# Who scales the probabilities and takes the sign bits: VectorE's work handed to GpSimd in an attention and two-layer feed-forward kernel

## The chip, the core and the metric

The kernel runs on one core of one Trainium2 chip. Every time below is device microseconds (us) of one execution; the figure of merit is the median of several executions. Engines are called as the profile calls them: PE is TensorE (PEld its weight loads), DVE is VectorE, ACT is ScalarE, POOL is GpSimd, SP is SyncE, which here only issues DMAs.

## What is computed

Two batches of 768 positions, 8 heads of 64: attention inside a band (the 96 last positions and 8 global ones) with a linear bias, then two feed-forward layers on the 1536 tokens, 512 wide, with 2048 hidden units. In the reference, cut to what matters:

```python
scores = scale * np.matmul(q, k.transpose(0, 1, 3, 2)) + bias      # kept where keep, else -1e9
scores = scores - np.max(scores, axis=-1, keepdims=True)
a = np.exp(scores)
a = a / (np.sum(a, axis=-1, keepdims=True) + 1e-09)
x = np.matmul(a, v)
h = np.maximum(x @ w_in, 0.0);  x = h * h @ w_out                  # layer 0
h = x @ w_in2;  g = np.where(h >= 1, h, np.where(h <= -1, 0.0, (h + 1) ** 2 / 4))
out = g @ w_out2                                                   # layer 1
```

The weights arrive as 64-bit floats. [...]

## The kernel before

**The order is planned.** The program records every operation with the engines that may do it, an estimated duration and a due time, and `Plan.emit` (L184) then simulates the engines by those estimates and writes the instructions out in the order in which the simulation started them. Nothing is decided when the program runs: each engine takes its list in order and waits on semaphores. Three rules of `emit` matter here. An operation that several engines can do goes to the one that the plan thinks done first. VectorE and GpSimd share one path to SBUF in the plan: an operation flagged `port` may not start before `port`, the end of the last flagged one, so that no two of them ever overlap. And where the plan sees TensorE idle for longer than FGAP = 300 ns in the early part, it puts in **fillers**, matmuls on a tile of zeros (`warm`, recorded at L1342 until the first feed-forward product, at L1344 after it) whose result nobody reads.

**Attention.** The 12 blocks of 128 queries are done in halves of four heads (`BandAttention.half`). A half is: products of q and k (L868), four times "add the mask, keep the minimum" on VectorE (L890) and the exponential with its sum on ScalarE (L895), the addition of 1e-9 to the four sums (L900) and their reciprocal (L902) on VectorE, four multiplications of the probabilities by it (`Plan.scale`: L153 on ScalarE, L155 on VectorE, L157 on GpSimd), transposes on TensorE (L918), their copies out of PSUM (L129, L130), and the products with v (L954). Probabilities and sums have three buffers (`pr`, `mn`), so that consecutive halves overlap.

**Weights.** A chunk is 128 hidden units of both matrices, loaded as two DMAs into one of two `raw` buffers (L462). Each half of it becomes 32-bit floats in `whole` by four operations (`Ffn.float32`): ScalarE multiplies the high words, read as floats, by 2^-112 (L153); VectorE shifts the result left by 3 (L470), puts in the top three bits of the low words (L473) and then the sign bits of the high words (L477). A copy to the reduced format of the matmuls (ScalarE, L129) and a subtraction for the rest (VectorE, L140) give the two parts of a slot. A `raw` buffer is free for its next DMA when L477 has read it. All 16 chunks of layer 0 are made while attention runs, those of layer 1 later (`prepare`, L492), for storage in HBM.

**Order of the large loops.** The first 8 halves of attention come alone; from about the ninth on, the feed-forward of finished tokens (L535, L733; at first in pieces of 256 tokens) runs in between; then layer 0 for the rest, then layer 1 (L652, with its own products).

```python
            if ways[engine][2]:
                t = max(t, port)
                port = t + ns
```

## Time and profile before

| | us |
|---|---|
| median of 3 runs (lowest to highest) | 614.76 (613.58 to 614.92) |
| the profiled execution | 613.96 |
| its span, first to last instruction | 612.2 |

| engine | busy us of the span | share |
|---|---|---|
| PE | 599.7 | 98% |
| DVE | 481.0 | 79% |
| ACT | 351.5 | 57% |
| POOL | 58.1 | 9% |

The profiled execution lies 1.8 us above its span and 0.8 us below the median. A busy share is an average over stages that have different limits, so it has to be read together with a table by stage. A busy TensorE is also not yet a useful one: the fillers count as busy.

### The profile page before, as it was taken

The page shows a single profiled execution, that of the slowest core. Times are in us where ns is not written, and L with a number is a line of the kernel's source. Part 1 is how long each engine was busy: PE and PEld are TensorE (multiplying, and loading weights), DVE is VectorE, ACT ScalarE, POOL GpSimd, SP SyncE. Part 2 cuts the span into 40 slices and gives each one's busy share as a digit, 9 for nine tenths or more (in the row PEclk, how much of TensorE's full clock was granted, in tenths as well). Part 3 has the DMA queues.
Part 4 walks back from the last instruction along what each step waited for, and adds up shares of the span by engine and source line. Part 5 has one row for each costly group of instructions (what it writes and reads, how often), then busy time and mean ns, then how long its engine had stood idle before and what let it go on. Part 6 is the DMA issues. An engine that isn't in the chain of part 4 may idle for free. (4 is left out here: it accounts for less than half of the span.)

```text
span 612.2 us, 9673 instructions
## 1 busy us (share of the span) xinstructions
PE 599.7 (98%) x3438; PEld 514.0 (84%) x3438; DVE 481.0 (79%) x1031; ACT 351.5 (57%) x731; POOL 58.1 (9%) x88
## 2 busy tenths in 40 slices
PE   8999999999999999999999999999999999999995
PEld 5778987878888888888888898888899999888884
DVE  7999999965638988898566389999897788887862
ACT  7898877765547766674447464545553444444331
POOL 4120111010001104233200000000000000000000
PEclk9999999999999999999999999999999999999999
DMA  8553544430114879988512202323220022223002
GB/s 303 166 185 118 186 147 154 150 121 22 38 36 124 272 235 304 359 321 283 193 68 70 94 27 69 118 73 107 82 96 1 35 104 96 96 94 96 26 2 108
DMA packets 25790, 79.24 MB, mean 129 GB/s; under 512 B 2948, under 2 KB 2948, under 8 KB 25732
## 3 DMA queue, kind: packets, MB, share of 16 engines
q1 hardware_dynamic: 25730, 78.52, 38.0%
q8 instruction: 29, 0.48, 0.3%
q14 instruction: 29, 0.24, 0.1%
q10 hardware_dynamic: 2, 0.00, 0.0%
HBM read 62.78 MB, written 15.73 MB: 128 GB/s over the span
## 5 line engine op out<-in xcount | busy, mean ns | idle before, releaser
L658 DVE TENSOR_TENSOR pr<-bank,pr 128x384 f32<-128x384 f32 x112 | 60.2, 554 | 23.4 <-PE bank L652 22.5
L140 DVE TENSOR_TENSOR g<-r,g 128x512 fp32r<-128x512 f32 (+2 forms) x74 | 48.9, 660 | 34.7 <-ACT g L129 33.8
L550 ACT ACTIVATE r<-bank 128x512 f32<-128x512 f32 (+1 forms) x52 | 29.2, 562 | 59.7 <-PE bank L535 58.9
L129 ACT ACTIVATE g<-r 128x512 fp32r<-128x512 f32 (+2 forms) x74 | 42.7, 577 | 24.9 <-DVE r L567 14.2
L895 ACT ACTIVATE pr<-pr,mn 128x256 f32<-128x256 f32 (+1 forms) x96 | 45.9, 480 | 4.6 <-DVE mn L890 4.2
L563 ACT ACTIVATE r<-pr,small 128x384 f32<-128x384 f32 x43 | 26.2, 615 | 32.8 <-DVE pr L658 32.7
L153 ACT ACTIVATE whole<-raw 128x512 f32<-128x512 f32 x52 | 33.9, 668 | 9.1 <-DMA raw<-in_moe_w_out_dram 3.2
L477 DVE SCALAR_TENSOR_TENSOR whole<-raw,whole 128x512 uint32<-128x512 uint32 x52 | 36.7, 712 | 0.4
L890 DVE CUSTOM_DVE_ANT_0 pr<-bank,m 128x256 f32<-128x256 f32 (+1 forms) x96 | 33.4, 397 | 4.2 <-PE bank L954 4.1
L473 DVE SCALAR_TENSOR_TENSOR whole<-raw,whole 128x512 uint32<-128x512 uint32 x52 | 35.9, 702 | 0.3
L157 POOL TENSOR_SCALAR pr<-pr,mn 128x256 f32<-128x256 f32 (+1 forms) x38 | 21.4, 570 | 120.3 <-DVE mn L902 57.9
L868 PEld LDWEIGHTS bank<-nat,nat 64*128 64x128 f32 x352 | 22.7, 190 | 7.6 <-issue 2.7
L565 DVE SCALAR_TENSOR_TENSOR r<-r 128x384 f32<-128x384 f32 x43 | 23.8, 556 | 5.9 <-ACT r L563 5.1
L868 PE MATMUL bank<-nat,nat 64*128 64x128 f32 x352 | 27.0, 288 | 1.3 <-DVE mn L890 1.2
L563 ACT ACTIVATE nat<-pr,small 128x384 f32<-128x384 f32 x21 | 12.9, 617 | 24.5 <-DVE pr L658 24.5
L470 DVE TENSOR_SCALAR whole<-whole 128x512 uint32<-128x512 uint32 x52 | 22.9, 448 | 4.0 <-ACT whole L153 3.7
L129 ACT ACTIVATE pr<-bank 128x512 f32<-128x512 f32 (+2 forms) x46 | 23.5, 521 | 3.4 <-PE bank L652 2.1
L567 DVE TENSOR_TENSOR r<-pr,r 128x384 f32<-128x384 f32 x43 | 23.8, 557 | 1.2
L954 PE MATMUL bank<-pr,nat 128*64 128x128 f32 x352 | 24.0, 277 | 0.6 <-DVE mn L890 0.3
L918 PE MATMUL bank<-ident,pr 128*128 128x128 f32 x176 | 23.9, 275 | 0.0
L954 PEld LDWEIGHTS bank<-pr,nat 128*64 128x64 f32 x352 | 19.7, 136 | 4.8 <-issue 2.0
L918 PEld LDWEIGHTS bank<-ident,pr 128*128 128x128 f32 x176 | 20.0, 140 | 2.8 <-issue 0.5
(347 smaller groups left out, 1753.6 us busy)
## 6 DMA issues: line engine op xcount, KB each, us to landing
raw<-in_moe_w_in_dram SPq DMA_DIRECT2D x32, 512.0 KB, 4.4
raw<-in_moe_w_out_dram SPq DMA_DIRECT2D x32, 512.0 KB, 4.8
whole<-sums SPq DMA_DIRECT2D x14, 512.0 KB, 3.3
kept<-whole SPq DMA_DIRECT2D x12, 512.0 KB, 6.3
whole<-kept SPq DMA_DIRECT2D x12, 512.0 KB, 3.3
whole<-kept SPq DMA_DIRECT2D x13, 384.0 KB, 3.1
sums<-pr SPq DMA_DIRECT2D x8, 512.0 KB, 5.8
nat<-in_k_dram SPq DMA_DIRECT2D x12, 256.0 KB, 3.7
```

The source lines that it names most:

```text
L129: ("act", ns_act(n) - 30 * psum, lambda: nc.scalar.activation(out=at(out), in_=in_, func=ACTF.Copy), False),
L140: ways = [("dve", ns_dve(n), lambda: nc.vector.tensor_tensor(out=at(out), in0=in_, in1=at(hi).bitcast(F32), op=ALU.subtract), not psum)]
L153: ("act", ns_act(n) + (0 if isinstance(by, float) else 107), lambda: nc.scalar.activation(out=out, in_=in_, func=ACTF.Copy, scale=by), False),
L473: op("dve", ns_dve(512), d + 0.2, lambda h=h: nc.vector.scalar_tensor_tensor(out=word[:, h], in0=low[:, h], scalar=29, in1=word[:, h], op0 ...
L477: op("dve", ns_dve(512), d + 0.3, lambda h=h: nc.vector.scalar_tensor_tensor(out=word[:, h], in0=high[:, h], scalar=0x80000000, in1=word[: ...
L563: op("act", ns_act(N) + 64, due, lambda: nc.scalar.activation(out=r, in_=h, func=ACTF.Relu, bias=self.half, scale=0.5), keys, [kr])
L658: op("dve", ns_dve(W), start + step[name] + 0.2 - G_LEAD, lambda: nc.vector.tensor_tensor(out=to, in0=area[kb], in1=in1, op=ALU.add), [("b ...
L868: nc.tensor.matmul(**c)
L890: op("dve", ns_dve(w), due, lambda e=e: nc.vector.tensor_tensor_reduce(out=pr[:, e, :w], in0=self.banks[kbs[e % 2]][:, e // 2 * 256:e // 2 ...
L895: op("act", ns_act(w) + 200, due, lambda e=e: nc.scalar.activation(out=pr[:, e, :w], in_=pr[:, e, :w], func=ACTF.Exp, bias=mn[:, e:e + 1], ...
L918: self.nc.tensor.transpose(self.banks[kbs[m]][:, o:o + P], pr[:, 2 * m + e, c * P:(c + 1) * P], self.ident)
L954: nc.tensor.matmul(**c)
```

## The change

The plan no longer keeps VectorE and GpSimd apart. A flagged operation of GpSimd is planned 1.3 times as long (SHARE) and marks its end in `port`; a flagged operation of VectorE that starts before that end is planned longer by what is left of it, at most 90 ns (GIVE). The rule by which VectorE passed over a flagged operation (PASS) is gone. Three pieces of work move: from block 2 on (half 4 on) all four multiplications of a half are GpSimd's, where ScalarE, VectorE and GpSimd shared them; the 1e-9 is added by GpSimd; and the sign bits are taken by GpSimd. For the last one the four operations on a half chunk become: ScalarE's as before; GpSimd multiplies the high words by 0.0, which leaves a zero with the sign, in place in `raw`; VectorE combines that with the top bits of the low words, in place in `raw`; VectorE shifts ScalarE's result by 3 and combines it with that. VectorE has two operations per half chunk where it had three.

```diff
-SCALE, SCALE0 = ("act", "dve", "pool"), ("dve", "pool")
-CONV = ("act",)
+SCALE, SCALE0 = ("pool",), ("dve", "pool")
+CONV, SIGN = ("act",), ("pool",)
...
-                    others = max(free[e], t, port if ways[e][2] else 0)
-                    own = max(t, port if ways[engine][2] else 0)
+                    others, own = max(free[e], t), t
...
             if ways[engine][2]:
-                t = max(t, port)
-                port = t + ns
+                if engine == "pool":
+                    ns *= SHARE
+                    port = t + ns
+                elif engine == "dve" and port > t:
+                    ns += min(GIVE, port - t)
...
-            op("dve", ns_dve(256), d + 0.1, lambda h=h: nc.vector.tensor_scalar(
-                out=word[:, h], in0=word[:, h], scalar1=3, scalar2=None, op0=ALU.logical_shift_left,
-            ), (), [(*kc, n)], port=True)
+            self.plan.scale(512, d, high[:, h].bitcast(F32), high[:, h].bitcast(F32), 0.0, [(*kc, n)], [(*kr, n)], engines=SIGN)
             op("dve", ns_dve(512), d + 0.2, lambda h=h: nc.vector.scalar_tensor_tensor(
-                out=word[:, h], in0=low[:, h], scalar=29, in1=word[:, h],
+                out=low[:, h], in0=low[:, h], scalar=29, in1=high[:, h],
                 op0=ALU.logical_shift_right, op1=ALU.bitwise_or,
-            ), [(*kr, n)], [(*kc, n)], port=True)
+            ), (), [(*kr, n)], port=True)
             op("dve", ns_dve(512), d + 0.3, lambda h=h: nc.vector.scalar_tensor_tensor(
-                out=word[:, h], in0=high[:, h], scalar=0x80000000, in1=word[:, h],
-                op0=ALU.bitwise_and, op1=ALU.bitwise_or,
+                out=word[:, h], in0=word[:, h], scalar=3, in1=low[:, h],
+                op0=ALU.logical_shift_left, op1=ALU.bitwise_or,
             ), [(*kr, n)], [(*kc, n)], port=True)
...
-        op("dve", 70, due + 0.1, lambda: nc.vector.tensor_scalar(
-            out=mn[:, 4:8], in0=mn[:, 4:8], scalar1=1e-9, scalar2=None, op0=ALU.add), (), sums, port=True)
+        op("pool", 150, due + 0.1, lambda: nc.gpsimd.tensor_scalar(
+            out=mn[:, 4:8], in0=mn[:, 4:8], scalar1=1e-9, scalar2=1.0, op0=ALU.add, op1=ALU.mult), (), sums)
```

Since the plan simulates with new costs, all engines get a new order. Three places of it follow. Line numbers of the changed kernel are 6 to 8 lower than those of before (L527 for L535, L725 for L733, L860 for L868, L892 and L894 for L900 and L902).

GpSimd, from the second half of block 1 on. `pr<-pr,mn` is a multiplication of probabilities (mn_77, 78 and 79 are the three buffers of the sums), `nat` a small copy of keys. Before:

```order
L157 TENSOR_SCALAR pr<-pr,mn_77 128x256 x3
L133 TENSOR_SCALAR nat_125<-nat_125 128x4x32
L157 TENSOR_SCALAR pr<-pr,mn_78 128x256 x3
L157 TENSOR_SCALAR pr<-pr,mn_79 128x256
L157 TENSOR_SCALAR pr<-pr,mn_77 128x256
```

Now, with the sign operations (`raw<-raw`) and the additions (`mn<-mn`) in the same queue:

```order
L157 TENSOR_SCALAR pr<-pr,mn_77 128x256 x2
L157 TENSOR_SCALAR raw_116<-raw_116 128x512
L157 TENSOR_SCALAR raw_117<-raw_117 128x512 x2
L157 TENSOR_SCALAR raw_116<-raw_116 128x512 x2
L157 TENSOR_SCALAR raw_117<-raw_117 128x512
L133 TENSOR_SCALAR nat_125<-nat_125 128x4x32
L892 TENSOR_SCALAR mn_78<-mn_78 128x4
L157 TENSOR_SCALAR pr<-pr,mn_78 128x256 x3
L892 TENSOR_SCALAR mn_79<-mn_79 128x4
```

One to three multiplications of a half have become four, and six sign operations stand before the first addition of block 2.

TensorE, after the first feed-forward product of chunk 1 (`slot1`), on 256 tokens. Before:

```order
L535 MATMUL bank_63<-x,slot1l 128x256
L535 MATMUL bank_63<-x,slot1h 128x256 x2
L535 MATMUL bank_63<-x,slot1l 128x256
L535 MATMUL bank_63<-x,slot1h 128x256
L1344 LDWEIGHTS warm
L1344 MATMUL bank_63<-warm 128x256
```

Now:

```order
L527 MATMUL bank_63<-x,slot1l 128x256
L527 MATMUL bank_63<-x,slot1h 128x256
L725 MATMUL bank_65<-g_120,slot0h 128x256
L725 MATMUL bank_65<-g_120,slot0l 128x256
L725 MATMUL bank_65<-g_120,slot0h 128x256
L725 MATMUL bank_66<-g_120,slot0h 128x256
```

Nine fillers in a row stood there before, and 21 at L1344 in all; now the second product of chunk 0 (`slot0`) follows, and of the later fillers two are left. The earlier ones, at L1342, go from 31 to 35.

SP, the loads of block 5 (`in_q`, `in_k`, `in_v`) beside those of a weight chunk. Before:

```order
L841 DMA nat_125<-in_k_dram 128x512
L841 DMA nat_127<-in_v_dram 128x512
L841 DMA nat_126<-in_q_dram 128x512
L965 DMA nat_127<-in_v_dram 32x512
L462 DMA raw_117<-in_moe_w_in_dram 128x1024
L462 DMA raw_117<-in_moe_w_out_dram 128x1024
```

Now:

```order
L456 DMA raw_117<-in_moe_w_in_dram 128x1024
L456 DMA raw_117<-in_moe_w_out_dram 128x1024
L833 DMA nat_126<-in_q_dram 128x512
L833 DMA nat_125<-in_k_dram 128x512
L833 DMA nat_127<-in_v_dram 128x512
```

The two weight DMAs, which wait until VectorE has done with `raw`, have moved ahead of the loads of block 5.

## Rows read from the trace of the kernel before

**Rows 1.** Busy time by stage (windows; columns in the second line).

```profile
core 0: us, PE busy (x) PEld busy (x) DVE busy (x) ACT busy (x) POOL busy (x), PEclk, DMA share, GB/s
0.00:21.60 21.60, 18.69 (x161) 13.38 (x161) 16.61 (x74) 16.63 (x55) 8.40 (x25) 1.00 0.67 239
21.60:55.00 33.40, 30.96 (x305) 26.57 (x304) 30.88 (x101) 28.37 (x81) 6.13 (x10) 1.00 0.56 188
55.00:75.00 20.00, 20.00 (x196) 18.93 (x195) 19.48 (x63) 17.17 (x51) 2.11 (x4) 1.00 0.46 154
75.00:125.00 50.00, 50.00 (x371) 40.28 (x369) 48.21 (x133) 37.61 (x99) 5.93 (x10) 1.00 0.47 150
125.00:605.00 480.00, 480.00 (x2414) 414.80 (x2412) 365.43 (x663) 251.35 (x446) 35.56 (x39) 1.00 0.35 118
605.00:612.20 7.20, 0.02 (x1) 0.00 (x0) 0.42 (x1) 0.38 (x1) 0.00 (x0) 0.86 0.27 97
```

**Rows 2.** The same windows for the tile `warm` alone: the fillers.

```profile
21.60:55.00 33.40, 3.40 (x23) 1.87 (x21) 0.00 (x0) 1.00 0.56 188
```

**Rows 3.** TensorE in order of time: start, length, operation, count, the wait before it.

```profile
31.02 0.60 PE L1344 MATMUL bank<-warm 128*128 128x256 bf16 x4 [0.47 <-ACT r L550]
32.20 0.38 PE L1344 MATMUL bank<-warm 128*128 128x256 bf16 x2 [0.59 <-DVE r L552]
33.77 0.83 PE L1344 MATMUL bank<-warm 128*128 128x256 bf16 x6
36.76 1.25 PE L918 MATMUL bank<-ident,pr 128*128 128x128 f32 x8
56.78 1.42 PE L868 MATMUL bank<-nat,nat 64*128 64x128 f32 x16
```

**Rows 4.** Groups of DVE, 21.6 to 55 us (count | busy us, mean ns | idle before).

```profile
L473 DVE SCALAR_TENSOR_TENSOR whole<-raw,whole 128x512 uint32<-128x512 uint32 x7 | 4.8, 686 | 0.0
L477 DVE SCALAR_TENSOR_TENSOR whole<-raw,whole 128x512 uint32<-128x512 uint32 x6 | 4.1, 677 | 0.0
L470 DVE TENSOR_SCALAR whole<-whole 128x512 uint32<-128x512 uint32 x6 | 2.5, 419 | 0.0
L155 DVE TENSOR_SCALAR pr<-pr,mn 128x256 f32<-128x256 f32 x4 | 1.6, 404 | 0.0
L140 DVE TENSOR_TENSOR slot3l<-whole,slot3h 128x512 fp32r<-128x512 f32 x2 | 1.4, 690 | 0.0
L900 DVE TENSOR_SCALAR mn<-mn 128x4 f32<-128x4 f32 x5 | 0.8, 166 | 0.1
```

**Rows 5.** Groups of POOL and ACT in the same stretch.

```profile
L157 POOL TENSOR_SCALAR pr<-pr,mn 128x256 f32<-128x256 f32 x8 | 5.3, 666 | 16.8 <-DVE mn L902 16.8
...
L153 ACT ACTIVATE pr<-pr,mn 128x256 f32<-128x256 f32 x8 | 3.6, 498 | 0.9 <-DVE mn L902 0.9
```

**Rows 6.** POOL in order of time: multiplications and a small copy, at three places.

```profile
9.43 0.74 POOL L157 TENSOR_SCALAR pr<-pr,mn 128x128 f32<-128x128 f32 x2 [0.61 <-DVE mn L902]
10.29 0.30 POOL L133 TENSOR_SCALAR nat<-nat 128x128 f32<-128x128 f32 x1
34.37 0.94 POOL L157 TENSOR_SCALAR pr<-pr,mn 128x256 f32<-128x256 f32 x1 [2.80 <-DVE mn L902]
57.12 0.54 POOL L157 TENSOR_SCALAR pr<-pr,mn 128x256 f32<-128x256 f32 x1 [5.48 <-ACT pr L129]
```

**Rows 7.** DVE in order of time, around the third row of group 6.

```profile
34.03 0.17 DVE L902 RECIPROCAL mn<-mn 128x4 f32<-128x4 f32 x1
34.12 0.66 DVE L477 SCALAR_TENSOR_TENSOR whole<-raw,whole 128x512 uint32<-128x512 uint32 x1
34.70 0.35 DVE L155 TENSOR_SCALAR pr<-pr,mn 128x256 f32<-128x256 f32 x1
34.96 0.88 DVE L140 TENSOR_TENSOR slot1l<-whole,slot1h 128x512 fp32r<-128x512 f32 x1
```

**Rows 8.** POOL and DVE in order of time, near 241 us.

```profile
240.56 1.12 POOL L503 TENSOR_TENSOR pr<-whole,whole 128x256 f32<-128x256 f32 x1 [8.32 <-DVE whole L477]
...
241.11 1.11 DVE L477 SCALAR_TENSOR_TENSOR whole<-raw,whole 128x512 uint32<-128x512 uint32 x1
```

**Rows 9.** SP's queue in order of time: the load of q of block 5.

```profile
41.84 0.43 SPq L841 DMA_DIRECT2D nat<-in_q_dram  x1
```

More of the change, by code (lines that the diff above doesn't have):

```diff
@@ L44 @@
 FROM = 25
-PASS = 1.0
+SHARE, GIVE = 1.3, 90
 HOLD, NEAR = 0.5, 1
@@ L219, in emit @@
             i = heapq.heappop(a)[1]
-            if port > t and engine == "dve" and ops[i][0]["dve"][2]:
-                other = min(((d, j) for d, j in a if not by[j] and not ops[j][0]["dve"][2]), default=None)
-                if other and other[0] < ops[i][1] + PASS:
-                    heapq.heappush(a, (ops[i][1], i))
-                    a.remove(other)
-                    heapq.heapify(a)
-                    i = other[1]
             if engine in ("act", "dve", "pool") and HOLD:
```

## The prediction

> **What bounds the kernel now.** I read the table by stage first. From 55 to 605 us TensorE is busy in every microsecond, at a granted clock of 1.00 [rows 1]: 550 of the 612.2 us are a solid block of matmuls which the change neither adds to nor takes from, so whatever VectorE, ScalarE or GpSimd gain there buys nothing as long as TensorE stays fed. From 605 us the last tiles leave; nothing of the change is there. What is left is the first 55 us. From 0 to 21.6 us TensorE is busy for 18.69, in good part with fillers, and from 21.6 to 55 us for 30.96 of 33.40 [rows 1], of which 3.40 are fillers again [rows 2]. So in that second stretch 33.40 - 30.96 + 3.40 = 5.8 us do no work. That is the purse this change can draw on. The reader is to see in the same table what TensorE is short of there: VectorE is at 30.88 of 33.40 us, ScalarE at 28.37, GpSimd at 6.13 [rows 1]. The waits say the same: fillers stand behind a ScalarE operation (0.47 us) and a VectorE one (0.59 us) of the feed-forward [rows 3]; the attention and weight work queued on these two engines holds up the next products. From 75 to 125 us VectorE is as full, 48.21 of 50.00, but TensorE has longer pieces of work there and doesn't wait [rows 1].
>
> **The change, part by part, for 21.6 to 55 us.**
>
> Off VectorE: the shift, 2.5 us; the multiplications, 1.6 us; the addition of 1e-9, 0.8 us [rows 4]: 4.9 us of 30.88. The two operations that stay on a half chunk are of the kind and size of the two that cost 686 and 677 ns [rows 4], so I give them the same. Off ScalarE: eight multiplications, 3.6 us of 28.37 [rows 5].
>
> Onto GpSimd: 4 + 8 multiplications beside its own 8 [rows 4, 5], six sign operations and five additions. An undisturbed multiplication of 128x256 takes 0.54 us and one of 128x128 half of 0.74 = 0.37 us [rows 6]. Going on by that step, a sign operation of 128x512 is 0.54 + 2 x 0.17 = 0.88 us (an estimate; ends 0.54, if size cost nothing, and 1.08, if it cost all). An addition on 128x4 lies between nothing and the 0.30 us of the small copy [rows 6]; I take 0.25, by its nearness to that row. Sum: 20 x 0.54 + 6 x 0.88 + 5 x 0.25 = 17.3 us of 33.4, about 52% busy where it was 18%. GpSimd has room for it as a queue.
>
> What GpSimd's work costs VectorE is not idle time but collisions. In the trace a GpSimd multiplication that starts at 34.37 while VectorE is in L477 (until 34.78) takes 0.94 instead of 0.54 us [rows 6, 7]; the VectorE subtraction that meets its end (34.96) takes 0.88 [rows 7] where its like takes 0.69 [rows 4], so 0.19 more. A longer, two-input GpSimd operation at 240.56 makes L477 1.11 us [rows 8] instead of 0.68, so 0.43 more. I read that as one at a time for operations with two SBUF inputs: 240.56 + 1.12 = 241.68 is GpSimd's end, and L477, begun at 241.11, ends 0.54 later. The Trainium skill says the same (SBUF — State Buffer, section "SBUF: two separate sides"): the pair of ports that VectorE and GpSimd share is an exclusive lock, and the loser waits in full. By that rule the plan's 90 ns (GIVE) is too little, and the new order is packed too tightly.
>
> How often? VectorE keeps some 23 such operations in the stretch (7 + 6 at L473 and L477 [rows 4], by which there are about 7 slot subtractions at L140, and I add 3 for the hidden layer). With GpSimd busy for 52% of the time, about 12 meet it. Two thirds of GpSimd's busy time are multiplications, one third signs: 8 x 0.19 + 4 x 0.43 = 3.2 us. At 90 ns each it would be 1.1 us. So VectorE's net relief is 4.9 - 3.2 = 1.7 us by the collisions that the rows show, and 3.8 us by the plan's allowance. Its ends are 4.9 us (no collision) and 4.9 - 23 x 0.43 = -5.0 us (every one, at the dear price). ScalarE's 3.6 us come without collisions, and TensorE waits for it as often as for VectorE. **I take -2.0 us** for the stretch, a little over VectorE's own 1.7 for what ScalarE adds, out of the 5.8 us of purse. The order shows where it would be collected: 19 of the 21 late fillers are gone, and six of them took 0.83 us, 0.14 each [rows 3], so 2.6 us of them.
>
> **From 0 to 21.6 us.** Here the first eight halves run alone and TensorE follows the chain scores, exponential, reciprocal, multiplication, transposes. The multiplications there keep their two engines; the addition goes to GpSimd and adds a trip: at 34.03 + 0.17 = 34.20 the reciprocal ends and GpSimd starts at 34.37 [rows 6, 7], 0.17 us for a handover, so about +0.17 and +0.25 - 0.17 for the longer operation, 0.25 us per half. The first sign operations come late in this stretch, before the last multiplications, and are about 0.46 us longer than the shift they replace. Against that VectorE sheds a few shifts and additions. The order puts in 35 early fillers for 31: four of 0.14 us [rows 3]. **I take +0.5 us**, with ends -0.7 (four additions of 0.17 us saved on the chain) and +1.5 (0.25 us on each of four halves that nothing covers, and 0.46 for the first chunk).
>
> **From 55 us on: 0.** VectorE sheds the same three kinds of work there and meets GpSimd as often; TensorE is full, and the cover is that weights and hidden tiles are made ahead of it. If that cover went, each late half chunk would show as TensorE idle time, which no row of before has. SP: the two weight DMAs now stand ahead of block 5's loads, behind VectorE's release of `raw`. In the trace that q is issued at 41.84 [rows 9] and first used at 56.78 [rows 3], 15 us; VectorE would have to be late by most of that, so I cost it at nothing. The sign operations of layer 1's weights come while TensorE is in layer 0, which doesn't read them.
>
> Sum: -2.0 + 0.5 = **-1.5 us**. Against the profiled execution's 613.96 us (span 612.2) that is **612.5 us**; this execution lies 0.8 us under the median of 614.76, so on the median's scale the same sum is 613.3.
>
> A cost that no row of before shows is VectorE writing every second word (`raw`, in place). Reading every second word costs nothing: L473 reads `raw` so and takes 686 ns, the dense L140 690 [rows 4]. I take nothing for the write as well. The Trainium skill speaks against it (Vector Engine (DVE) Microarchitecture Reference, section "Measured stream behaviour on trn2"): full rate wants runs of two adjacent words, and single words cost about 0.65 cycle per element on reading and writing alike. By that rule the read in L473 should have been dearer too, which the row denies; a write at the page's price would be an estimated 0.35 us more per operation, 2.1 us for six, and would eat the gain.
>
> **Rivals.**
>
> *The plan is right and the purse is nearly emptied.* If collisions cost VectorE what the plan allows or less, the order holds, and the stretch gives up to VectorE's 4.9 us: -4.9 + 0.5, so 609.6 us. For it: the order, with two late fillers left. Against it: the 0.19 and 0.43 us of [rows 7, 8].
>
> *The relief is eaten.* Collisions, or the strided write, cost VectorE all that it sheds; fillers turn into plain waits of the same length: 0 + 0.5 in the first stage, at 614.0 to 614.5 us. For it: the exclusive use that the rows show. Against it: ScalarE's share.
>
> *Slower: GpSimd as the only scaler is late, and the transposes wait.* Four multiplications of a half now follow each other; the order was made with 1.3 x 457 = 594 ns for one (the plan's formula). Undisturbed they take 0.54, disturbed 0.94 us [rows 6]; at the middle, 0.75, a half is 4 x 0.15 = 0.6 us later than planned. In before, the shared multiplications ended at 34.37 + 0.94 = 35.31 [rows 6] and the transposes began at 36.76 [rows 3], a margin of 1.45 us, but the new order has no fillers left to take up lateness. Five halves of the stretch at 0.6 us are +3.1 us: -2.0 + 0.5 + 3.1 gives 615.6 us; at 0.94 throughout it would be 619. It decides from a mean multiplication of about 0.66 us on, where 5 x 4 x 0.07 = 1.4 us eat the gain. The mean in this stretch before, with few neighbours, is already 666 ns [rows 5].
>
> That the change doesn't do what it says can be left out: the order shows the moved operations.
>
> **How the numbers follow.** The forecast has 0.38, the emptied purse 0.22, the eaten relief 0.16, the slower case 0.24. A measurement of this kernel can tell about 0.2%, 1.2 us, from no change. The forecast's 1.5 us is just beyond that, so 0.29 of its 0.38 count as faster and 0.09 as the same; with the purse 0.51 faster, with the eaten relief 0.25 the same, 0.24 slower. The range: down to 609.5, the emptied purse; up to 616.0, which takes in the middle of the slower case and leaves out its dear end.
>
> **What would show it.** Right: from 21.6 to 55 us fewer fillers, TensorE's waits there no longer than before, VectorE near 29 us for the same work, L157 near 0.65 us, the block after 55 us still without a gap, and the end of the first stage up to half a us later. The first rival: VectorE's two-input operations at 0.69 on average despite GpSimd. The slower one: TensorE or its weight loads waiting at L910 for GpSimd's L157, and gaps after 55 us. A mean of the first VectorE operation on `raw` (L465) much above 0.69 us with no GpSimd beside it would show the strided write. The prediction is wrong if the time that moves lies after 55 us, or in the first stage by more than 1.5 us.

## The result and the profile after

The changed kernel takes **621.72 us** (median of 6 executions, 620.13 to 626.39), the kernel before 614.49 us on the same chip (6 executions, 613.58 to 614.92): a ratio of **1.0133, 95% interval 1.0106 to 1.0161**. It is slower, by about 7 us. The forecast was 612.5 us with a range of 609.5 to 616.0: wrong in sign, and outside its range. The profiled execution took 621.39 us with a span of 619.5, 7.3 us more than the 612.2 of before.

The table by stage answers to [rows 1]; its columns are the same (time and number of instructions per engine, then TensorE's granted clock, DMA share, GB/s).

```profile
0.00:21.60 21.60, 19.69 (x162) 14.08 (x163) 15.65 (x68) 16.30 (x53) 12.25 (x31) 1.00 0.71 253
21.60:55.00 33.40, 28.56 (x263) 24.52 (x261) 30.73 (x83) 25.60 (x71) 20.26 (x31) 0.95 0.54 169
55.00:75.00 20.00, 19.94 (x206) 18.51 (x205) 19.41 (x55) 16.57 (x47) 13.61 (x20) 1.00 0.66 215
75.00:125.00 50.00, 49.92 (x362) 40.06 (x362) 37.47 (x107) 33.55 (x94) 24.98 (x41) 1.00 0.42 143
125.00:605.00 480.00, 476.93 (x2404) 410.47 (x2403) 357.51 (x612) 247.10 (x436) 70.90 (x96) 1.00 0.35 115
```

Two things are new. The block after 55 us has gaps: 476.93 of 480.00 in its long row, where before it was 480.00. And from 21.6 to 55 us the granted clock is 0.95. The same view in steps of 25 us shows the place of the gaps:

```profile
200.00:225.00 25.00, 25.00 (x112) 20.68 (x111) 21.98 (x30) 17.70 (x31) 10.20 (x12) 1.00 0.70 232
225.00:250.00 25.00, 23.33 (x102) 18.67 (x100) 18.23 (x26) 14.44 (x24) 8.30 (x10) 1.00 0.79 255
250.00:275.00 25.00, 23.86 (x104) 19.41 (x105) 20.25 (x27) 13.77 (x22) 15.90 (x18) 1.00 0.97 331
275.00:300.00 25.00, 24.73 (x108) 19.86 (x107) 23.58 (x37) 14.86 (x27) 13.74 (x15) 1.00 0.93 319
```

A full window holds 112 matmuls, 25/112 = 0.223 us each. The three windows hold 10 + 8 + 4 = 22 too few: **4.9 us**. (Counted as idle time it is only 1.67 + 1.14 + 0.27 = 3.1 us, since the profile models where a matmul ends; the weight loads, which show the gaps too, waited for 5.2.) The other part of the loss lies ahead of it. The attention's products of probabilities with v are the last of the attention; the view of one line shows when the first and the last of them start, here in the kernel before and then in the changed one (operation, count, min/median/max ns, first and last start):

```profile
L954 PE MATMUL bank<-pr,nat x352: 272/273/323, 11.2 to 171.0; 128*64 128x128 f32 x176
```

```profile
L946 PE MATMUL bank<-pr,nat x352: 272/273/324, 12.2 to 173.6; 128*64 128x128 f32 x176
```

So **2.6 us** are lost by 173 us, 4.9 from 225 to 300, and 2.6 + 4.9 = 7.5 is within 0.2 us of the 7.3 of the span.

**What TensorE waits for from 225 to 300 us.** The waits of PE in 200 to 300 us of the changed kernel are a single row (total in us, times, longest), and its weight loads have the same one:

```profile
PE bank L725 <- DVE g L140: 3.1, 4, 1.2
```

```profile
PEld bank L725 <- DVE g L140: 5.2, 5, 1.6
```

`g` is the hidden tile that the second product of the feed-forward reads; VectorE's subtraction makes its low half. One such place in order of time (start, length, operation, count, idle before and what ended it):

```profile
225.03 1.84 POOL L157 TENSOR_SCALAR raw<-raw 128x512 f32<-128x512 f32 x2 [2.25 <-ACT whole L153]
225.23 1.13 DVE L469 SCALAR_TENSOR_TENSOR m<-m,raw 128x512 uint32<-128x512 uint32 x1
225.87 0.39 PE L725 MATMUL bank<-g,slot7l 128*128 128x512 f32 x1
226.28 1.12 DVE L140 TENSOR_TENSOR g<-r,g 128x512 fp32r<-128x512 f32 x1
227.46 0.72 PE L725 MATMUL bank<-g,slot7h 128*128 128x512 f32 x2 [1.20 <-DVE g L140]
```

GpSimd makes sign bits from 225.03 to 226.87. A weight step of VectorE (L469) meets them and takes 1.13 us in place of 0.68; behind it in VectorE's list stands `g`, which meets them too and takes 1.12; TensorE stands for 1.20 us. The weight step was in no hurry: TensorE first reads the slot that it is made for (slot6) at 264.75. The groups of VectorE over the whole span have the meetings in their means (count | busy, mean ns | idle before). L465 and L469 are VectorE's two steps on a half chunk, L140 is the subtraction. Operations of their kind and size took 677 to 690 ns from 21.6 to 55 us of before [rows 4], and over its whole span 702 (L473), 712 (L477) and, for `g`, 757.

```profile
L465 DVE SCALAR_TENSOR_TENSOR raw<-raw 128x512 uint32<-128x512 uint32 x64 | 52.0, 827 | 15.1 <-POOL raw L157 15.0
L469 DVE SCALAR_TENSOR_TENSOR whole<-whole,raw 128x512 uint32<-128x512 uint32 x52 | 37.5, 736 | 1.0
L140 DVE TENSOR_TENSOR g<-r,g 128x512 fp32r<-128x512 f32 x44 | 35.5, 808 | 21.8 <-ACT g L129 21.2
```

The first row also shows a wait that the kernel before doesn't have: 15.0 us in which VectorE, which takes its list in order, stands until a sign step is done.

That `g` is slow is not enough for a hole, though. The same group from 225 to 300 us alone, in the kernel before, in the changed one and in give_all, an experiment told below (the same kernel with another price in the plan, and no holes):

```profile
L140 DVE TENSOR_TENSOR g<-r,g 128x512 fp32r<-128x512 f32 x14 | 12.0, 857 | 8.1 <-ACT g L129 8.0
L140 DVE TENSOR_TENSOR g<-r,g 128x512 fp32r<-128x512 f32 x14 | 13.1, 938 | 0.0
L140 DVE TENSOR_TENSOR g<-r,g 128x512 fp32r<-128x512 f32 x14 | 11.5, 823 | 4.6 <-ACT g L129 4.6
```

The kernel before has slow ones too, at 857 ns on average, but there VectorE was early: it stood 8.0 us waiting for ScalarE's half of `g`. In the changed kernel it never waits for that half (0.0). It comes to each of the 14 only after that half is ready, since other work stands ahead of it in its list.

**What happens ahead of 55 us.** The first feed-forward product starts at 23.81 us, where it was 21.64 before. In order of time, in the changed kernel:

```profile
18.68 2.78 POOL L157 TENSOR_SCALAR raw<-raw 128x512 f32<-128x512 f32 x3
19.81 2.19 DVE L465 SCALAR_TENSOR_TENSOR raw<-raw 128x512 uint32<-128x512 uint32 x2 [0.56 <-POOL raw L157]
21.93 0.68 DVE L469 SCALAR_TENSOR_TENSOR whole<-whole,raw 128x512 uint32<-128x512 uint32 x1
22.64 0.63 ACT L129 ACTIVATE slot0h<-whole 128x512 fp32r<-128x512 f32 x1 [1.92 <-DVE whole L469]
23.18 0.58 ACT L129 ACTIVATE x<-bank 128x512 fp32r<-128x512 f32 x1
23.81 0.39 PE L527 MATMUL bank<-x,slot0h 128*128 128x256 f32 x1 [1.70 <-ACT x L129]
```

Three sign steps in a row on GpSimd, two VectorE steps that take 2.19 us beside them (at 686 ns each [rows 4] it would be 1.4), ScalarE standing 1.92 us for them with a tile of x queued behind, and TensorE 1.70 us for that. Then the clock (same columns as the table by stage):

```profile
21.60:24.00 2.40, 0.70 (x6) 0.39 (x5) 2.40 (x5) 1.27 (x3) 0.00 (x0) 1.00 0.30 72
24.20:27.60 3.40, 3.18 (x17) 2.85 (x18) 2.65 (x5) 1.37 (x4) 1.01 (x1) 0.53 0.93 296
27.60:55.00 27.40, 24.48 (x244) 21.18 (x242) 25.48 (x75) 22.76 (x66) 19.25 (x30) 1.00 0.51 163
```

After the gap (0.70 us busy of 2.40) the granted clock is 0.53 on average over 3.4 us, its lower level (1.2 GHz) for nearly all of them: by an estimate 0.47 x 3.4 = 1.6 us lost. The late fillers, on the other hand, nearly went: 0.90 us of them from 21.6 to 55 us against 3.40 [rows 2].

```profile
21.60:55.00 33.40, 0.90 (x7) 0.31 (x5) 0.00 (x0) 0.95 0.54 169
```

So the late start (2.2) and the clock (1.6) stand against 2.5 us of fillers saved: 1.3 us lost. The 1.3 us that are left to the 2.6 were not traced one by one. TensorE has further waits from 21 to 56 us: 1.0 us for GpSimd's multiplications (at L910), 0.9 for VectorE's mask step and 0.9 for the low half of a slot. The first of them, over the whole span (total, times, longest):

```profile
PE bank L910 <- POOL pr L157: 1.3, 3, 0.7
```

### The profile page after: what moved, and what is told of

It reads as the page before. It is cut to its first block, busy times and chain, and to the rows that moved or that the text cites. A ratio compares the mean times of both kernels' runs of the same rounds, so it can differ in the third digit from the quotient of the medians.

```text
span 619.5 us, 9731 instructions
## 1 busy us (share of the span) xinstructions
PE 602.5 (97%) x3423; PEld 513.5 (83%) x3423; DVE 463.9 (75%) x928; ACT 341.9 (55%) x704; POOL 142.0 (23%) x218
## 5 line engine op out<-in xcount | busy, mean ns | idle before, releaser
L140 DVE TENSOR_TENSOR g<-r,g 128x512 fp32r<-128x512 f32 (+2 forms) x74 | 51.6, 697 | 25.5 <-ACT g L129 24.8
L157 POOL TENSOR_SCALAR raw<-raw 128x512 f32<-128x512 f32 x64 | 50.0, 791 | 76.2 <-ACT whole L153 54.0
L465 DVE SCALAR_TENSOR_TENSOR raw<-raw 128x512 uint32<-128x512 uint32 x64 | 52.0, 827 | 15.1 <-POOL raw L157 15.0
L157 POOL TENSOR_SCALAR pr<-pr,mn 128x256 f32<-128x256 f32 (+1 forms) x88 | 56.5, 658 | 10.4 <-DVE mn L894 9.8
L469 DVE SCALAR_TENSOR_TENSOR whole<-whole,raw 128x512 uint32<-128x512 uint32 x52 | 37.5, 736 | 1.0
L860 PEld LDWEIGHTS bank<-nat,nat 64*128 64x128 f32 x352 | 23.3, 196 | 6.3 <-issue 3.9
L557 DVE SCALAR_TENSOR_TENSOR r<-r 128x384 f32<-128x384 f32 x43 | 23.8, 556 | 5.9 <-ACT r L555 5.1
L860 PE MATMUL bank<-nat,nat 64*128 64x128 f32 x352 | 27.9, 295 | 0.1
L910 PE MATMUL bank<-ident,pr 128*128 128x128 f32 x176 | 25.3, 277 | 1.5 <-POOL pr L157 1.3
L910 PEld LDWEIGHTS bank<-ident,pr 128*128 128x128 f32 x176 | 19.9, 140 | 6.2 <-POOL pr L157 2.7
L559 DVE TENSOR_TENSOR r<-pr,r 128x384 f32<-128x384 f32 x43 | 23.8, 557 | 1.2
```

The costliest lines, as they stand in the source:

```text
L140: ways = [("dve", ns_dve(n), lambda: nc.vector.tensor_tensor(out=at(out), in0=in_, in1=at(hi).bitcast(F32), op=ALU.subtract), not psum)]
L157: ("pool", ns_pool2(n) + (0 if isinstance(by, float) else 141), lambda: nc.gpsimd.tensor_scalar(out=out, in0=in_, scalar1=by, scalar2=1.0, ...
L465: op("dve", ns_dve(512), d + 0.2, lambda h=h: nc.vector.scalar_tensor_tensor(out=low[:, h], in0=low[:, h], scalar=29, in1=high[:, h], op0= ...
L469: op("dve", ns_dve(512), d + 0.3, lambda h=h: nc.vector.scalar_tensor_tensor(out=word[:, h], in0=word[:, h], scalar=3, in1=low[:, h], op0= ...
L860: nc.tensor.matmul(**c)
L910: self.nc.tensor.transpose(self.banks[kbs[m]][:, o:o + P], pr[:, 2 * m + e, c * P:(c + 1) * P], self.ident)
```

## The experiments

Eighteen kernels ran, each beside the kernel before on the same chip. Ratios are to that kernel. The change has four parts: the new rule of the plan (a meeting of VectorE and GpSimd is allowed, at most GIVE = 90 ns are charged to VectorE), the sign bits on GpSimd, the multiplications on GpSimd alone, and the addition there. The theories at the start were: the sign steps hold VectorE up (T1); GpSimd is late as the only scaler (T2, the slower rival of the prediction); the new rule makes an order that is too tight, whoever does the work (T3).

### Which part costs

**sign_back** and **scale_back** undo one part each in the changed kernel; **old_rule** undoes the rule; **rule_alone** has nothing but the rule.

```diff
 sign_back: float32() of before in place of the changed one
 scale_back:
-SCALE, SCALE0 = ("pool",), ("dve", "pool")
+SCALE, SCALE0 = ("act", "dve", "pool"), ("dve", "pool")
 old_rule: emit() and PASS of before, the rest as changed
 rule_alone: emit(), SHARE and GIVE of the change, the rest as before
```

Expected of sign_back: 

> The changed kernel with the weights' sign bits taken by VectorE again (the four operations of before on a half chunk); rule of the plan, scaling and addition as changed. Theory 1 (GpSimd's sign operations hold up VectorE's two-input operations, at the start of the feed-forward and while layer 1's weights are made, 225 to 300 us): 613 to 616 us, with 112 matmuls in each of the windows 225:250, 250:275 and 275:300 again. Theory 2 (GpSimd as the only scaler makes attention late): still 619 us or more, the lost time before 175 us. Theory 3 (the new rule of the plan packs the order too tightly, whoever does the work): 617 us or more.

Measured: 616.70 us, 1.0038 (1.0025 to 1.0051), between the ranges of T1 and T3. The windows from 225 to 300 us hold 112, 112 and 107 matmuls.

Expected of scale_back: 

> The changed kernel with the multiplications shared by ScalarE, VectorE and GpSimd again; sign bits, addition and rule as changed. Theory 1: 619 to 622 us, with 102 to 108 matmuls per 25 us from 225 to 300 us as in the changed kernel. Theory 2: 614 to 616 us. Theory 3: 617 us or more.

Measured: 622.08 us, 1.0125 (1.0108 to 1.0142), with 106, 107 and 106 matmuls in these windows: nothing is gained. T2 doesn't carry the loss of the changed kernel, though that has 1.3 us of the waits it speaks of (above); with the scaling given back 0.8 us of them are left.

Expected of old_rule: 

> The changed kernel's division of work under the old rule of the plan (GpSimd and VectorE never side by side, PASS back). Theory 1: the work still collides or queues, so 617 us or more, since VectorE waits for GpSimd's sign operation in either order. Theory 2: 618 us or more. Theory 3: 613 to 615 us, since the plan then allows for the exclusive use.

Measured: 615.98 us, 1.0023 (1.0011 to 1.0034), between the range of T3 (up to 615) and that of T1 (from 617), with 112 matmuls in all three windows. All of the moved work, under the old rule, costs about a sixth of what the change costs (0.0023 of 0.0133).

Expected of rule_alone: 

> The kernel before with the new rule of the plan alone (SHARE, GIVE, no PASS), all work where it was. Theory 1: 613 to 616 us, since GpSimd has little to collide with. Theory 2: 613 to 616 us. Theory 3: 617 us or more.

Measured: 618.73 us, 1.0068 (1.0045 to 1.0090), 112 in all three windows; its loss lies ahead of 200 us.

What follows: the rule costs by itself, ahead of 200 us, and nearly all of the holes from 225 to 300 us need the rule and the sign steps together (sign_back keeps 5 of the 22). The late first feed-forward product needs both as well: it starts at 22.5 us in sign_back, 22.1 in old_rule and 22.9 in rule_alone, but at 23.8 in scale_back as in the changed kernel. T1 and T3 each had a half.

### Is it the price in the plan?

The trace has 0.43 us for a meeting [rows 8], the plan 0.09 at most. If VectorE's steps look nearly free to the plan beside GpSimd, it sees no reason to put `g` ahead of a weight step. **give_0**, **give_430** and **give_all** change this number alone; **rule_full**, **scale_full** and **scale_back_full** set it to 1000 where parts are undone.

```diff
-SHARE, GIVE = 1.3, 90
+SHARE, GIVE = 1.3, 0        # give_0;  430: give_430;  1000: give_all
 rule_full: rule_alone with GIVE = 1000
 scale_full: sign_back with GIVE = 1000
 scale_back_full: scale_back with GIVE = 1000
```

Expected of give_0: 

> The changed kernel with the price of a meeting taken away in the plan (GIVE 0 ns in place of 90): the other end of the scale on which 1000 ns took 1.0012 of the time before and 90 ns took 1.0133. If the plan's price is what decides: no better than the changed kernel, 621 to 626 us, with at most 108 of TensorE's rows in each 25 us from 225 to 300 us. If 90 ns is as good as nothing (the trace shows 430 ns and more for a meeting): the same as the changed kernel within 1 us. If the time falls under 620 us, the price is not what decides.

Measured: 624.15 us, 1.0152 (1.0131 to 1.0173); 111, 108 and 98 matmuls. The interval overlaps that of the changed kernel.

Expected of give_430: 

> The changed kernel with the price of a meeting as the trace of before has it, about 430 ns (GIVE 430 in place of 90). 0 ns took 1.0152, 90 ns 1.0133, 1000 ns 1.0012. If the time falls with the price as it comes near to the measured one: 615 to 617 us with no hole from 225 to 300 us. If only the full wait keeps VectorE's steps apart from TensorE's needs: 618 us or more.

Measured: 616.10 us, 1.0021 (1.0007 to 1.0035); 112, 112 and 112.

Expected of give_all: 

> The changed kernel with one constant changed: a VectorE step that meets a GpSimd step is planned to wait the whole of it out (GIVE 1000 ns in place of 90). The work of each engine stays as in the changed kernel; only the plan's price differs. If the changed kernel loses because its plan prices a meeting at 90 ns or less where the trace shows about 0.4 us and more: 225 to 300 us shows some 112, 112 and 112 of TensorE's rows per 25 us (changed kernel 102, 104, 108) and the time falls to 616 us or less. If it is the absence of any wait of GpSimd for VectorE in the plan that matters, or the moved work itself, whatever the price: 619 to 622 us.

Measured: **614.97 us, 1.0012** (1.0002 to 1.0021). The holes are closed (windows of give_all):

```profile
225.00:250.00 25.00, 25.00 (x112) 20.72 (x111) 19.93 (x25) 14.03 (x23) 13.55 (x15) 1.00 0.83 271
250.00:275.00 25.00, 25.00 (x112) 20.68 (x112) 20.86 (x28) 15.44 (x28) 13.81 (x16) 1.00 0.93 322
275.00:300.00 25.00, 25.00 (x112) 20.72 (x111) 20.70 (x30) 13.03 (x22) 15.28 (x17) 1.00 0.89 301
```

And it is not that VectorE meets GpSimd less. The weight steps take as long as in the changed kernel or longer; `g` alone is quicker, 736 ns for 808 (757 in the kernel before), and VectorE is in time for it again, as the rows from 225 to 300 us above show (groups of VectorE in give_all, whole span):

```profile
L465 DVE SCALAR_TENSOR_TENSOR raw<-raw 128x512 uint32<-128x512 uint32 x64 | 51.7, 823 | 13.9 <-POOL raw L157 13.9
L469 DVE SCALAR_TENSOR_TENSOR whole<-whole,raw 128x512 uint32<-128x512 uint32 x52 | 41.1, 797 | 1.1
L140 DVE TENSOR_TENSOR g<-r,g 128x512 fp32r<-128x512 f32 x44 | 32.4, 736 | 24.7 <-ACT g L129 24.1
```

In order of time, near the place shown above (give_all):

```profile
224.41 1.16 POOL L157 TENSOR_SCALAR raw<-raw 128x512 f32<-128x512 f32 x1 [1.90 <-ACT whole L153]
225.60 0.70 DVE L465 SCALAR_TENSOR_TENSOR raw<-raw 128x512 uint32<-128x512 uint32 x1 [0.55 <-POOL raw L157]
226.20 0.68 DVE L140 TENSOR_TENSOR g<-r,g 128x512 fp32r<-128x512 f32 x1
226.79 2.24 POOL L157 TENSOR_SCALAR raw<-raw 128x512 f32<-128x512 f32 x2 [1.23 <-ACT whole L153]
227.41 1.12 DVE L140 TENSOR_TENSOR slot6l<-m,slot6h 128x512 fp32r<-128x512 f32 x1
```

`g` stands ahead of the step that waits, in GpSimd's pause, and takes 0.68; the meeting falls on a subtraction for weights (1.12), which TensorE first reads at 259.56. The work on each engine is that of the changed kernel. So the price decides the order, and the order the 7 us. The first feed-forward product, too, starts earlier, at 22.7 us.

Expected of rule_full: 

> The kernel before, its division of work untouched, under the new rule with the full price (GIVE 1000 ns). With 90 ns the new rule alone took 1.0068. If that was the price: 614 to 615 us (0.999 to 1.001), and TensorE does not stand still for more than 1 us at one place after 25 us. If it was the rule's form (GpSimd never waits for VectorE in the plan, and no VectorE step is put back): 616.5 us or more.

Measured: 615.34 us, 1.0012 (1.0001 to 1.0024). The rule itself comes down from 1.0068 with the price; a remainder of 0.1% stays, with one wait of 1.8 us for VectorE and one of 1.9 for a DMA of v in the profile, more than the 1 us expected.

Expected of scale_full: 

> The new rule with the full price (GIVE 1000 ns), GpSimd as the only one to scale probabilities from block 2 on and adding the 1e-9, the sign bits on VectorE. With 90 ns this took 1.0038; the full price gave 7 us to the changed kernel. If the scaling on GpSimd relieves VectorE and ScalarE where the plan knows the price: 613 us or less, under the kernel before. If relief and meetings cancel, as in the changed kernel under the full price (1.0012): 614.5 to 615.5 us. If scaling on GpSimd alone costs, as under the old rule (1.0045): 616 us or more.

Measured: 615.88 us, 1.0024 (1.0014 to 1.0034): between two of the cases, no gain.

Expected of scale_back_full: 

> The changed kernel under the full price (GIVE 1000 ns) with the multiplications shared again among ScalarE, VectorE and GpSimd; sign bits and the addition of 1e-9 stay on GpSimd. With GpSimd as the only scaler this took 1.0012. If having only one engine to scale costs a little (GpSimd is late for TensorE twice, 1.1 us, in that kernel): 613 to 614 us, as fast as the kernel before or faster. If sharing costs VectorE more than it gives: 615 us or more.

Measured: 615.55 us, 1.0013 (0.9998 to 1.0028): no different from give_all. With the full price no difference shows between one scaler and three.

### Whose meeting, and what the gap does

**sign1_back** has the sign bits of layer 1's weights alone back on VectorE; **act_sign** has them made by ScalarE, whose result in this run is not the reference's, so its weights lack their proper signs and only its time is used; **fill_gap** puts 15 filler products ahead of the first feed-forward product.

```diff
 sign1_back: in float32(), "if layer == 0:" the changed steps, "else:" those of before
 act_sign:
-CONV, SIGN = ("act",), ("pool",)
+CONV, SIGN = ("act",), ("act",)
 fill_gap: in emit(), ahead of the first feed-forward matmul
+            if i == self.first and self.filler:
+                fills += [(t - 1 - n, 1, warmer) for n, warmer in enumerate([self.filler] * 15)]
```

Expected of sign1_back: 

> The changed kernel with the sign bits of layer 1's weights alone back on VectorE (layer 0's stay on GpSimd). If the loss from 225 to 300 us comes from GpSimd's sign steps meeting VectorE's steps there: 112 rows of TensorE in each 25 us of it, 4.9 us less than the changed kernel, some 616.5 to 617 us, and what is lost ahead of 175 us stays (the first feed-forward product again starts near 23.8 us). If that stretch is late because of what happened ahead of it, or of layer 0's signs: no better than 620 us.

Measured: 618.83 us, 1.0070 (1.0053 to 1.0087); 112, 112 and 112 matmuls from 225 to 300 us. The holes go as expected; the time fell by 2.9 us only, where 4.9 was expected. The order ahead of the holes changed too: its profile, of an execution that took 621.55 us, has a wait of 2.7 us for ScalarE's copy of a probability tile at 79 us, followed by some 7 us at the clock's lower level. How much of this the faster executions (down to 617.39 us) have, no trace shows.

Expected of act_sign: 

> The changed kernel (price 90 ns) with the sign bits made by ScalarE in place of GpSimd; VectorE still has two steps per weight half in place of three. ScalarE and VectorE were not seen to hold each other up in these traces. If the holes from 225 to 300 us come from GpSimd's sign steps holding VectorE's steps up: 112 of TensorE's rows in each 25 us there, 4.9 us less than the changed kernel, 615.5 to 617.5 us. If they come from the new chain itself (VectorE's last step waits for two steps of others in a row): they stay, 620 us or more. ScalarE has 0.42 us and more of work added for each of 64 halves, so the stages ahead of 75 us may lose up to 2 us where it is the busier engine.

Measured: 616.74 us, 1.0041 (1.0025 to 1.0056), 112 in all three windows at the price of 90 ns. The chain is as long as in the changed kernel; it is GpSimd's sign steps beside VectorE that make the holes.

Expected of fill_gap: 

> The changed kernel with 15 more filler products on TensorE right ahead of the first feed-forward product, in the gap in which TensorE waits for the weights. If the granted clock of 0.50 from 24.3 to 27.7 us in the changed kernel follows from that idle gap: the clock stays 1.00 from 21.6 to 55 us and the time is about 1.7 us less, some 620 us. If the drop has another reason, the clock falls as before and the time stays within 0.5 us of 621.7; fillers that hold the product up would make it later still, by up to 1.5 us.

Measured: 622.37 us, 1.0137 (1.0119 to 1.0154), the same as the changed kernel. The clock stays 1.00 where it had fallen, and falls after the next gap instead (windows of fill_gap):

```profile
24.20:27.60 3.40, 3.15 (x31) 2.72 (x31) 3.40 (x7) 2.21 (x5) 1.54 (x2) 1.00 0.90 286
33.00:35.00 2.00, 0.97 (x6) 0.77 (x7) 2.00 (x8) 2.00 (x9) 1.73 (x2) 1.00 0.82 277
35.00:39.00 4.00, 4.00 (x23) 3.83 (x22) 3.31 (x6) 2.31 (x5) 3.83 (x6) 0.57 0.39 122
```

So filling the gap took the lower clock away from there; that an idle stretch goes ahead of it again fits. The lower clock costs something where it comes, but it is not the cause of the loss. Two of fill_gap's four executions had a mean granted clock of 0.998 over the whole span, as the profile of before has, and took 621.69 and 622.01 us. And scale_back's profile has no such stretch, though TensorE is busy for 0.69 of the same 2.40 us, and its time is that of the changed kernel.

### Why there is no gain even at the right price

give_all has 18 us less on VectorE than before (462.8 us busy over the span against 481.0; the prediction had 4.9 us of relief from 21.6 to 55 us), and gains nothing. Either that relief is worth nothing, or something eats it. **no_shift_old** takes VectorE's shift away and adds nothing (the weights' exponents are wrong); **no_sign_full** and **no_sign_old** leave the sign step out; **old_scale** and **old_sign** move one part each under the old rule.

```diff
 no_shift_old: kernel before
-            op("dve", ns_dve(256), d + 0.1, lambda h=h: nc.vector.tensor_scalar(
-                out=word[:, h], in0=word[:, h], scalar1=3, scalar2=None, op0=ALU.logical_shift_left,
-            ), (), [(*kc, n)], port=True)
 no_sign_full: give_all;  no_sign_old: old_rule
-            self.plan.scale(512, d, high[:, h].bitcast(F32), high[:, h].bitcast(F32), 0.0, [(*kc, n)], [(*kr, n)], engines=SIGN)
 ...          (VectorE's next step now waits for ScalarE's, as the sign step did)
 old_scale: old_rule with float32() of before
 old_sign: kernel before with float32() as changed, SIGN = ("pool",)
```

Expected of old_scale: 

> The kernel before, under its old rule, with GpSimd as the only one to scale probabilities from block 2 on and adding the 1e-9; sign bits stay on VectorE. The old rule with all of the moved work took 1.0023 of the time before. If the sign steps make that cost: 1.000 here, 614 to 615 us. If scaling on GpSimd alone makes it: 1.002 or more, 615.7 us or more. If scaling on GpSimd is a gain that the sign steps ate: 613 us or less.

Measured: 617.14 us, 1.0045 (1.0026 to 1.0063). Its profile has TensorE's transposes wait for GpSimd, which they don't in the kernel before (there only 0.3 us of their weight loads):

```profile
PE bank L918 <- POOL pr L157: 2.4, 5, 0.7
```

Expected of no_shift_old: 

> The kernel before, under its old rule, with VectorE's first weight step (the shift by 3, 0.41 us for each of 64 halves) left out, so the weights come out with a wrong exponent and this part is not done. It takes 26 us of work off VectorE and adds none anywhere, so no meeting can eat the relief. If VectorE's work is what the stages ahead of 75 us wait for: 612.5 us or less. If not: 613.5 to 615 us, the same as before, and the 5.8 us from 21.6 to 55 us were not to be had by relieving VectorE.

Measured: **610.93 us, 0.9933** (0.9910 to 0.9956). From 21.6 to 55 us TensorE and its fillers (second row: the tile `warm` alone):

```profile
21.60:55.00 33.40, 32.18 (x315) 28.06 (x313) 31.39 (x100) 30.31 (x88) 6.49 (x9) 1.00 0.58 189
...
21.60:55.00 33.40, 0.96 (x8) 0.37 (x5) 0.00 (x0) 1.00 0.58 189
```

32.18 - 0.96 = 31.22 us of work where before did 30.96 - 3.40 = 27.56 [rows 1, 2]: 3.7 us more, and 3.4 us less on the medians. The relief is worth a great deal where it brings no meetings. (Leaving the shift out also takes a step out of the chain of every weight; the two were not told apart.)

Expected of no_sign_full: 

> The changed kernel under the full price (GIVE 1000 ns) with the sign step left out altogether, so the weights lack their proper sign bits and this part of the computation is not done; all else as in the changed kernel. GpSimd has 50 us less to do and VectorE still has two steps in place of three. The full price with the sign step took 1.0012. If the relief of VectorE from 21.6 to 55 us is worth the 2.0 us forecast, or more, once fewer meetings eat it: 612.5 us or less. If what bounds these stages is not VectorE's amount of work: 614 to 615 us, as with the sign step.

Measured: 615.95 us, 1.0024 (1.0004 to 1.0043), above both ranges: none of it is left under the new rule with scaling on GpSimd, and leaving the sign step out is no faster than doing it (give_all, 1.0012).

Expected of no_sign_old: 

> Old rule, GpSimd as the only one to scale from block 2 on and adding the 1e-9, VectorE with two steps per weight half and the sign step left out altogether (the weights lack their proper sign bits, that part is not done). VectorE has the relief that took 0.9933 in the kernel with the shift left out, and about as many steps; what differs is the scaling and the addition on GpSimd. If these cost what they cost under the old rule with the signs on VectorE (1.0045): 0.9933 + 0.0045, some 613.5 to 614.5 us. If they take the relief whole, as under the new rule's full price (1.0024): 615.5 us or more. If they cost nothing: 611.5 us or less.

Measured: 613.91 us, 0.9990 (0.9979 to 1.0000), the first of the cases: scaling on GpSimd costs about what it cost with the signs on VectorE.

Expected of old_sign: 

> The kernel before, under its old rule and with the multiplications shared as before, with the sign bits alone moved to GpSimd (VectorE two steps in place of three). Leaving VectorE's shift out under the old rule, with nothing added, took 0.9933 (3.4 us less); all of the moved work under the old rule took 1.0023. If the sign steps are cheap enough where GpSimd waits for VectorE in the plan: 611 to 613.3 us, a version faster than both kernels. If the meetings and waits that they bring cost as much as the relief: 614 to 615.5 us.  If they cost more: 616 us or more.

Measured: 616.38 us, 1.0031 (1.0020 to 1.0042). With fillers taken off, its TensorE does 28.72 - 4.90 = 23.82 us of work from 21.6 to 55 us, 3.7 less than before (its median is only 1.9 us longer, so this difference is not kept whole):

```profile
21.60:55.00 33.40, 28.72 (x281) 24.66 (x281) 28.79 (x87) 26.33 (x75) 12.99 (x16) 1.00 0.52 178
...
21.60:55.00 33.40, 4.90 (x33) 2.77 (x31) 0.00 (x0) 1.00 0.52 178
```

Put in a row, each step adding one part:

| kernel | ratio | step |
|---|---|---|
| shift taken off VectorE, old rule (no_shift_old) | 0.9933 | -0.0067 |
| and GpSimd as only scaler, with the addition (no_sign_old) | 0.9990 | +0.0057 |
| and the sign bits on GpSimd (old_rule) | 1.0023 | +0.0033 |
| and the new rule at 90 ns (the change) | 1.0133 | +0.0110 |
| the same at 1000 ns (give_all) | 1.0012 | -0.0121 |

The parts don't add up in every order (the sign bits alone cost 1.0031 - 0.9933 = 0.0098 on top of the relief), but each of them eats relief in this one. Every edit makes the plan write a new order for all engines, and each version ran in one order only. How far the steps of 0.1 to 0.6% in this table are the order's chance was not tested; no_sign_full, which has less to do than give_all and is not faster, suggests that some of it is. The fall from 90 to 1000 ns doesn't rest on one pair: it repeats in rule_alone and rule_full (1.0068 to 1.0012), scale_back and scale_back_full (1.0125 to 1.0013) and, by less and not clear of the noise, in sign_back and scale_full (1.0038 to 1.0024). How the cost of scaling on GpSimd divides between meetings and the longer queue there was not settled; with the new rule's holes in place, giving the scaling back gains nothing. No version here beats the kernel before with the whole computation done.

## Why the prediction was wrong, step by step

- **"From 55 us on: 0" is the step that failed.** "The cover is that weights and hidden tiles are made ahead of it": before, it held, in this kernel it doesn't. The plan charges 90 ns at most where a meeting took 0.44 to 0.45 us at 225 us, so VectorE is later than planned with every meeting and in the end late for TensorE: its 8.0 us of waiting ahead of `g` from 225 to 300 us fell to 0.0. It cost 4.9 us. The text had the sentence on which this turns: the 90 ns are too little, and the new order is packed too tightly. It stood there by the Trainium skill's rule (SBUF — State Buffer, section "SBUF: two separate sides") that the loser waits in full. The trace agrees, with 1.12 us in place of 0.68 for the steps above. The prices of 0, 430 and 1000 ns show it with 1.0152, 1.0021 and 1.0012 (give_0, give_430, give_all). But I drew its consequence for 21.6 to 55 us alone, and as VectorE time, not as lateness.
- **From 21.6 to 55 us, -2.0.** The gain did not come. The purse of 5.8 us was there: no_shift_old takes 3.7 out of it. The meetings were sized well enough as VectorE's time: its groups in this stretch exceed those of [rows 4] by some 2.7 us (eight steps of L465 at 772 ns and eight of L469 at 757, for 686 and 677, and the subtractions), where 3.2 was forecast. VectorE was busy for 30.73 us all the same, not near 29. What was left out is which step a meeting hits: VectorE works its list in order, so a weight step that waits for GpSimd makes whatever stands behind it late, TensorE's own tiles among them, and 3.2 us of VectorE time is not a bound for that. TensorE did 28.56 - 0.90 = 27.66 us of work there against 27.56, with 3.4 us of it at the lower clock, so by an estimate 1.6 us less than that at full clock.
- **From 0 to 21.6 us, +0.5, ends -0.7 and +1.5.** The first feed-forward product is 2.2 us later, outside the ends. "0.46 for the first chunk" took the sign steps one by one; three in a row beside two VectorE steps, with ScalarE's copy of x queued behind the wait for the weights, made 1.70 us of wait for TensorE.
- **The clock** was in no term: it was 1.00 in every row up to 605 us [rows 1], and by the estimate above 1.6 us are lost after the gap that the late start makes.
- **The slower rival** (GpSimd as the only scaler is late, 615.6) came out on the right side, but its mechanism is a small part of the loss. The mean multiplication from 21.6 to 55 us took 0.76 us, beyond the 0.66 from which it was to decide, and TensorE waited for it for 1.0 us there and 1.3 in all, where 3.1 were counted. But scale_back, with the scaling given back, is as slow as the change. Under the old rule these waits are 2.4 us (old_scale).
- **The price of a meeting** was right: 0.43 for VectorE [rows 8], 0.44 in give_all at 227.41. The lengths on GpSimd were sized too high for work that meets nobody and came out near by the meetings: the least sign step took 0.64 us, not 0.88, the least multiplication of 128x256 0.47, not 0.54; their means in the changed kernel are 0.79 and 0.68. GpSimd was busy for 20.26 us from 21.6 to 55, where 17.3 was forecast.
- **The write of every second word, costed at nothing,** was right: 0.70 us for L465 at 225.60 in give_all, with GpSimd idle, beside 0.68 for the dense subtraction after it. The Trainium skill's dearer single words (Vector Engine (DVE) Microarchitecture Reference, section "Measured stream behaviour on trn2") don't show here.
- **The queue of loads past raw** was no part of the loss: a wait of TensorE for a load stands in none of the rows of the changed kernel from 21.6 to 55 us.

## What to carry to other kernels

Where a plan orders the work of engines that share a path, the price it sets on a meeting decides which step gets hit, and a price of a fifth of the measured one can cost more than the move could gain: here 7 us, with the same work on every engine. Before moving work to the other engine of such a pair, take work of that kind out altogether once; that gain (here 3.4 us for VectorE's shift) is what the meetings and waits of the moved work have to stay under. A block in which TensorE never waits is no proof of slack: ask how early its inputs are made, not only whether they are. Here the slack showed as VectorE's own wait ahead of `g`: 8.0 us before, none after.

## What the runs showed that was not expected

- The granted clock fell to its lower level for 3 to 7 us in seven of the twenty profiles of this study (the changed kernel, sign_back, rule_alone, fill_gap, sign1_back, old_scale, give_0), each time after TensorE had been waiting (busy for 0.70 of 2.40 us in the changed kernel, 0.69 of 2.90 in sign1_back). By an estimate a hole can thus cost 1.6 to 3.4 us more (0.47 x 3.4 in the changed kernel; 0.48 x 7.1 in sign1_back, at 0.52 from 81.9 to 89.0 us). Not each does: scale_back has the same gap as the changed kernel ahead of the feed-forward and keeps 1.00. What tells them apart was not settled. Nor is the kernel before free of it, though its profile is: of its 100 executions beside the experiments, 12 had a mean granted clock of 0.995 or less over the span, with a median of 615.6 us, and the other 88 one of 614.2.
- Two steps of VectorE per half chunk are cheaper in time than three were, but not by the whole step that went: over the whole span of the changed kernel they take 827 and 736 ns, 1.56 us in all, against 702 + 712 + 448 ns = 1.86 us in the kernel before. Of the 0.45 us of the shift 0.30 are saved; the two steps that stay take the rest, 0.15 us, with the meetings in their means.
